# Block-causal attention with a feed-forward layer on one core: rows first, heads second, in the loads of the first batch's q and k

## The chip, the cores and the metric

The kernel runs on one core of a Trainium2 chip. The metric is the device time of one execution in microseconds (us), as the median of several runs. One further execution was recorded by the hardware profiler; all rows below come from it.

## The reference

```python
# q, k, v: (8, 8, 576, 64) float32;  w_in: (512, 2048), w_out: (2048, 512)
scores = (q @ k^T) / sqrt(64)
mask   = (row // 64) >= (column // 64)          # causal in blocks of 64
attn   = softmax(where(mask, scores, -1e9))
x      = (attn @ v), heads side by side          # (4608, 512)
h      = x @ w_in
out    = (h * clip(h + 3, 0, 6) / 6) @ w_out     # (4608, 512)
```

## The kernel before

The work is cut into 32 slots: 8 batches times 4 pairs of heads. A slot's attention runs in 9 blocks of 64 query rows; its two heads sit on the lower and the upper 64 partitions. The feed-forward layer runs beside it, in 12 pieces of 384 tokens, as each piece's attention is finished.

The first four slots (batch 0) are done in float32, all others in split float16. Only the float32 slots are touched here. For each of them q and k are loaded in two parts by `qk_load32`: the first three blocks (192 rows of either head) into a tile `qf`, the other six (384 rows) into a tile `qr`. That makes 16 transfers in all: q and k, two parts, four slots. A partition of the tile holds `nt` neighbouring rows of one head (3 in `qf`, 6 in `qr`). In the kernel before, head 0 fills partitions 0 to 63 and head 1 partitions 64 to 127.

`qk_prep32` turns q and k, so that the 64 features lie on partitions: for each of the `nt` rows of a partition and each head, one product of that head's 64 partitions with a 64x64 piece of the identity matrix `ident`, written with a step of `nt` columns into a PSUM tile (`qt_0`, `qt_1` from `qf`; `qt_0r`, `qt_1r` from `qr`; the names carry 1 for k and 0 for q). A copy then moves the PSUM tile to `qkf`, from which the scores `sf` are computed (`s_pair32`), the softmax rows `pf`, their transposes `pt`, and the products with v, which also carry the name `pf` (`pv_group32`).

All transfers go through the queue of SyncE (SP), except a few of the first ones, which ScalarE issues. The weights arrive in 32 transfers of 512 KB into staging tiles (`rawi`, `rawo`, or a part of `x`), and ScalarE, GpSimd and VectorE turn them into float32 there (`exi`, `exo`, `sgi`, `sgo`) before they are split. The tile `qf` has two buffers, so the third slot's load of `qf` waits for the first slot's products.

The order of the instructions on each engine is fixed by a written-out table; the steps `AS`, `RT` and others only name the places. Every recorded operation carries the line L414 (the recorder's `emit`), so that the rows below are told apart by the names of tiles. On TensorE 40 products with a tile of zeros (`warm`) are spread over the first stretch.

Of the kernel before, what the change touches and what calls it, by code (L numbers as in the profile page):

```python
# [17 lines left out]
P = 128  # L18
# [29 lines left out]
AQ = ("sync", "scalar")  # L48
# [23 lines left out]
BLK = 64  # L72
# [345 lines left out]
def kernel(  # L418
# [113 lines left out]
    ident = wpool.tile([P, P], F32, tag="ident", name="ident")  # L532
# [309 lines left out]
    def qk_load32(n, rest=False):  # L842
        nt = NTR if rest else NTA
        if rest:
            t = natp.tile([P, 2, nt, D], F32, tag="qk", bufs=2, name=f"qr{n}")
        else:
            t = attp.tile([P, 2, nt, D], F32, tag="vhl", bufs=2, name=f"qf{n}")
        c0, c1 = (T0, S) if rest else (0, T0)
        for s, src in enumerate((q, k)):
            nc.load(  # L850
                t[:, s].rearrange("p t d -> p (t d)"),
                src[0, 2 * n:2 * n + 2, c0:c1].rearrange("h (p t) d -> h p (t d)", t=nt), AQ,
            )
        qn[n] = t

    def qk_prep32(n, rest):


        t = qn.pop(n)
        if not rest:  # L860

            if n < 3:
                o = attp.tile(
                    [P, 2 * S], F32, tag="qks" if n == 2 else "qkT", bufs=1 if n == 2 else 2,
                    name=f"qkf{n}",
                )
                qkT[n] = o[:, :S], o[:, S:]
            else:
                qkT[n] = [
                    attp.tile([P, NJ * 2 * P], F16, tag="phl2", bufs=3, name=f"qkf{n}_{i}").bitcast(F32)[:, :S]  # L870
                    for i in range(2)
                ]
        kT, qT = qkT[n]
        c0, c1 = (T0, S) if rest else (0, T0)
        pss = []
        for s in (1, 0):
            if rest and not QTH:
                ps = ps_s.tile([P, 512], F32, tag="s", name=f"qt{n}_{s}r")
            else:
                ps = ps_h.tile([P, S - T0], F32, tag="h", name=f"qt{n}_{s}")  # L880
            nt = NTR if rest else NTA
            nc.joint = "qt", n, s, rest
            for u in range(nt):
                for h in range(2):
                    hb = slice(h * BLK, (h + 1) * BLK)
                    nc.tensor.matmul(
                        ps[hb, u:nt * BLK:nt], t[hb, s, u], ident[hb, hb], start=True, stop=True
                    )
            nc.joint = None
            pss.append(ps)  # L890
        nc.scaled(kT[:, c0:c1], pss[0][:, :c1 - c0], 1.0, "AV")
        nc.scaled(qT[:, c0:c1], pss[1][:, :c1 - c0], D ** -0.5, "AV")
# [671 lines left out]
    def line(points, x):  # L1564

        for (x0, y0), (x1, y1) in zip(points, points[1:]):
            if x <= x1 or (x1, y1) == points[-1]:
                return y0 + (y1 - y0) * (x - x0) / (x1 - x0)
# [7 lines left out]
    for n in range(NPAIR):  # L1576
        t = AS[n]
        at(t, qk_load32, n, lead=AL)
        at(t, v_load, n, lead=AVL)
        at(t, qk_prep32, n, 0)  # L1580
        for b in ((0,), (1, 2)):
            at(t + (1 + b[0]) * U, s_pair32, n, *b)
        for i in range(GB):
            at(t + (1 + i) * U + TA, t_block32, n, i)
        at(t + GB * U + TA + PV0, pv_group32, n, 0)

    for n in range(NPAIR):
        t = RT[n]
        at(t - QR, qk_load32, n, True, lead=RL - QR)
        at(t - QR, qk_prep32, n, 1)  # L1590
        at(AS[3] + 0.1 + 0.1 * n, v_max, n)
        for i in range(2 * GB):
            if i % 2 == 0:
                at(t + i * RS, s_pair32, n, GB + i, GB + i + 1)
            at(t + i * RS + TR, t_block32, n, GB + i)
        for g in (1, 2):
            at(t + (g * GB - 1) * RS + TR + PR, pv_group32, n, g)

    for n in range(NPAIR, NSLOT):
        t, d = line(AT, n), line(AT, n + 1) - line(AT, n)  # L1600
# [97 lines left out]
```

## Time and profile before

| what | value |
|---|---|
| median of 3 runs | 1001.54 us (1000.66 to 1006.18) |
| the profiled execution, its own time | 1003.29 us |
| its span, from the first to the last instruction | 1001.5 us |
| TensorE busy | 964.0 us (96%) |
| VectorE busy | 834.5 us (83%) |
| ScalarE busy | 658.6 us (66%) |
| GpSimd busy | 124.7 us (12%) |
| mean granted TensorE clock | 0.984 of 2.4 GHz |

The span is shorter than the execution's time by 1.8 us, which lie around the first and the last instruction. Busy shares are averages over the span. TensorE's idle time, 37.5 us in all, is not spread evenly: the page's slices of 25 us show it to be mostly in the first five.

### The profile page before, as it was taken

The page shows a single profiled execution, that of the slowest core. Times are in us where ns is not written, and L with a number is a line of the kernel's source. Part 1 is how long each engine was busy: PE and PEld are TensorE (multiplying, and loading weights), DVE is VectorE, ACT ScalarE, POOL GpSimd, SP SyncE. Part 2 cuts the span into 40 slices and gives each one's busy share as a digit, 9 for nine tenths or more (in the row PEclk, how much of TensorE's full clock was granted, in tenths as well). Part 3 has the DMA queues.
Part 4 walks back from the last instruction along what each step waited for, and adds up shares of the span by engine and source line. Part 5 has one row for each costly group of instructions (what it writes and reads, how often), then busy time and mean ns, then how long its engine had stood idle before and what let it go on. Part 6 is the DMA issues. An engine that isn't in the chain of part 4 may idle for free.

```text
span 1001.5 us, 31335 instructions
## 1 busy us (share of the span) xinstructions
PE 964.0 (96%) x12625; PEld 676.5 (68%) x12625; DVE 834.5 (83%) x2366; ACT 658.6 (66%) x1638; POOL 124.7 (12%) x337
## 2 busy tenths in 40 slices
PE   4878999999999999999999999999999999999998
PEld 3656676667777867666667766776666666677775
DVE  1666889999899989999988888989887798978774
ACT  1665889997787887878766676677766553243422
POOL 1343641100001000000001000100100101000000
PEclk7997999999999999999999999999999999999999
DMA  2667677888979998889998968795895550000000
GB/s 86 184 201 214 192 142 141 158 144 172 178 128 177 196 184 141 161 174 162 152 161 145 150 125 143 144 158 117 134 170 100 96 100 17 2 33 3 33 3 33
DMA packets 406706, 129.05 MB, mean 129 GB/s; under 512 B 393504, under 2 KB 396064, under 8 KB 406560
## 3 DMA queue, kind: packets, MB, share of 16 engines
q1 hardware_dynamic: 405628, 126.59, 65.9%
q8 instruction: 99, 1.62, 0.7%
q10 hardware_dynamic: 932, 0.46, 0.2%
q14 instruction: 47, 0.39, 0.1%
HBM read 45.09 MB, written 9.44 MB: 54 GB/s over the span
## 4 chain that ended last, share of the span: by engine, by line
PE 73%; DMA 3%; DVE 2%; ACT 1%; issue 0%; SPq 0%; ACTq 0%; DVEq 0%
PE o L414 31%; PE h L414 25%; PE s L414 6%; PE m L414 5%; PE pv L414 5%; DMA pT<-phl 1%; DMA qkT<-qks 1%; DVE g L414 0%; DMA vnat<-in_v_dram 0%; SPq L414 0%; DMA out_dram<-osb 0%; DVE p L414 0%; PE o_2b L414 0%; ACT p L414 0%; DVE r L414 0%
## 5 line engine op out<-in xcount | busy, mean ns | idle before, releaser
L414 PE MATMUL o<-wout,g 128*64 128x512 f16 (+2 forms) x3336 | 416.5, 379 | 0.4 <-ACT osb L414 0.4
L414 PE MATMUL h<-x,win 128*64 128x384 f16 (+2 forms) x3952 | 363.4, 319 | 2.3 <-DVE hu L414 1.6
L414 PEld LDWEIGHTS <-win 128*64 128x64 f16 (+1 forms) x4440 | 244.4, 110 | 85.5 <-DVE hu L414 1.9
L414 PEld LDWEIGHTS <-g 128*64 128x64 f16 x3360 | 193.8, 110 | 119.2 <-issue 0.6
L414 ACT ACTIVATE r<-h,eg,sh 128x384 f32<-128x384 f32 (+1 forms) x192 | 112.3, 597 | 88.8 <-PE h L414 83.3
L414 ACT ACTIVATE p<-p,st 128x128 f32<-128x128 f32 (+8 forms) x252 | 139.1, 553 | 32.6 <-DVE st L414 31.8
L414 DVE SCALAR_TENSOR_TENSOR phl<-p,st,phl 128x256 f16<-128x256 f32 (+4 forms) x252 | 145.8, 588 | 6.2 <-ACT phl L414 4.6
L414 DVE CUSTOM_DVE_ANT_0 p<-s,none,esc 128x64 f32<-128x64 f32 (+7 forms) x252 | 120.3, 486 | 15.3 <-PE s L414 11.2
L414 DVE SCALAR_TENSOR_TENSOR g<-r,g 128x384 f16<-128x384 f32 (+1 forms) x192 | 105.6, 554 | 9.9 <-ACT g L414 8.5
L414 ACT ACTIVATE phl<-p,st 128x128 f16<-128x128 f32 (+4 forms) x166 | 95.3, 593 | 22.1 <-DVE st L414 18.1
L414 DVE SCALAR_TENSOR_TENSOR r<-r,eg,h 128x384 f32<-128x384 f32 (+1 forms) x160 | 93.6, 587 | 15.8 <-ACT r L414 15.1
L414 PE MATMUL s<-qkT 128*64 128x512 f16 (+7 forms) x1120 | 99.8, 287 | 0.3 <-DMA qkT<-qks 0.3
L414 PEld LDWEIGHTS <-vhl 128*64 128x64 f16 x1680 | 73.0, 110 | 18.0 <-issue 2.2
L414 PE MATMUL pv<-pT,vhl 128*64 128x192 f16 (+2 forms) x1680 | 82.7, 233 | 1.5 <-DMA pT<-phl 1.4
L414 ACT ACTIVATE g<-r 128x384 f16<-128x384 f32 (+1 forms) x109 | 53.5, 497 | 34.0 <-DVE r L414 15.7
L414 PEld LDWEIGHTS <-qkT 128*64 128x64 f16 x1120 | 55.8, 110 | 25.6 <-issue 0.8
L414 POOL MEMSET p<- 128x64 f32 x140 | 20.7, 163 | 327.5 <-DVE phl L414 288.8
L414 ACT ACTIVATE r<-hf,eg,sh 128x192 f32<-128x192 f32 (+1 forms) x48 | 26.8, 593 | 49.8 <-DVE hf L414 49.6
L414 ACT ACTIVATION_READ_ACCUMULATOR p<-p,st 128x1 f32 x252 | 47.7, 189 | 0.0
L414 DVE SCALAR_TENSOR_TENSOR qks<-qk,rs_q,qks 128x576 f16<-128x576 f32 x56 | 45.5, 815 | 0.7
L414 PE MATMUL m<-x,ws 128*64 128x192 f16 x768 | 39.7, 246 | 0.0
L414 PEld LDWEIGHTS <-ws 128*64 128x64 f16 x768 | 34.0, 110 | 5.5 <-issue 0.2
(206 smaller groups left out, 1110.8 us busy)
## 6 DMA issues: line engine op xcount, KB each, us to landing
out_dram<-osb SPq DMA_DIRECT2D x34, 256.0 KB
vnat<-in_v_dram SPq DMA_DIRECT2D x63, 128.0 KB
qk<-in_q_dram SPq DMA_DIRECT2D x28, 288.0 KB
qk<-in_k_dram SPq DMA_DIRECT2D x28, 288.0 KB
rawo<-in_moe_w_out_dram SPq DMA_DIRECT2D x13, 512.0 KB
x<-in_moe_w_in_dram SPq DMA_DIRECT2D x9, 512.0 KB
rawi<-in_moe_w_in_dram SPq DMA_DIRECT2D x7, 512.0 KB
pT<-phl SPq DMA_TRANSPOSE x140
```

The lines of the kernel that those rows point to most:

```text
L414: getattr(eng, method)(*args, **kw)
```

## The change

Both edits concern the first batch alone. The load names the rows' dimension ahead of the heads': the partition of row group p of head h becomes 2p + h, where it was 64h + p. A transfer moves the same bytes in the same number of pieces. The products that turn q and k then take all 128 partitions of the tile, and choose the head by the columns of the identity matrix: every second one, beginning with h. A product with the identity's columns of one head has zeros for the rows of the other.

```diff
@@ qk_load32
         for s, src in enumerate((q, k)):
             nc.load(
                 t[:, s].rearrange("p t d -> p (t d)"),
-                src[0, 2 * n:2 * n + 2, c0:c1].rearrange("h (p t) d -> h p (t d)", t=nt), AQ,
+                src[0, 2 * n:2 * n + 2, c0:c1].rearrange("h (p t) d -> p h (t d)", t=nt), AQ,
             )
@@ qk_prep32
                 for h in range(2):
                     hb = slice(h * BLK, (h + 1) * BLK)
                     nc.tensor.matmul(
-                        ps[hb, u:nt * BLK:nt], t[hb, s, u], ident[hb, hb], start=True, stop=True
+                        ps[hb, u:nt * BLK:nt], t[:, s, u], ident[:, h:P:2], start=True, stop=True
                     )
```

The order of instructions on every engine and every queue is the same before and after; only the operands of the 16 transfers and of the 384 products differ.

## Rows read from the trace of the kernel before

**Rows 1.** The page: span, TensorE's busy time, clock in 40 slices of 25 us.

```profile
span 1001.5 us, 31335 instructions
...
PE 964.0 (96%) x12625; PEld 676.5 (68%) x12625; DVE 834.5 (83%) x2366; ACT 658.6 (66%) x1638; POOL 124.7 (12%) x337
...
PEclk7997999999999999999999999999999999999999
```

**Rows 2.** Timeline of TensorE, 0 to 130 us: groups that begin after idle time.

```profile
start us, us, engine line op out<-in xcount [idle before <-releaser]
1.05 3.83 PE L414 MATMUL warm<-zero 128*128 128x256 f16 x19 [1.05 <-DVE zero L414]
15.43 1.55 PE L414 MATMUL qt<-ident,qf 64*64 64x64 f32 x24 [10.55 <-DMA qf<-in_q_dram]
17.55 0.80 PE L414 MATMUL qt<-ident,qf 64*64 64x64 f32 x10 [0.57 <-DMA qf<-in_k_dram]
...
24.02 0.56 PE L414 MATMUL qt<-ident,qf 64*64 64x64 f32 x12 [1.21 <-DMA qf<-in_q_dram]
...
29.49 0.91 PE L414 MATMUL qt_1r<-ident,qr 64*64 64x64 f32 x24 [1.76 <-DMA qr<-in_k_dram]
...
34.70 1.29 PE L414 MATMUL qt<-ident,qf 64*64 64x64 f32 x24 [2.94 <-DMA qf<-in_q_dram]
...
53.16 0.92 PE L414 MATMUL qt_1r<-ident,qr 64*64 64x64 f32 x24 [2.44 <-DMA qr<-in_k_dram]
...
60.81 0.43 PE L414 MATMUL pr<-rd,halves 128*128 128x64 f32 x2 [3.15 <-POOL rd L414]
...
84.04 1.54 PE L414 MATMUL qt_0r<-ident,qr 64*64 64x64 f32 x24 [4.12 <-DMA qr<-in_q_dram]
...
113.62 0.91 PE L414 MATMUL qt_0r<-ident,qr 64*64 64x64 f32 x24 [1.56 <-DMA qr<-in_q_dram]
```

**Rows 3.** Windows: engines' busy us (x instructions), then clock, DMA share, GB/s.

```profile
2.00:3.00 1.00, 1.00 (x7) 0.69 (x6) 0.00 (x0) 0.07 (x1) 0.06 (x1) 1.00 0.79 155
...
5.00:11.00 6.00, 0.00 (x0) 0.00 (x0) 0.00 (x0) 0.00 (x0) 0.00 (x0) 0.73 0.13 49
...
13.00:15.00 2.00, 0.00 (x0) 0.00 (x0) 0.00 (x0) 0.00 (x0) 0.00 (x0) 0.50 0.97 253
...
84.00:95.00 11.00, 10.96 (x111) 9.09 (x112) 5.29 (x12) 5.76 (x13) 6.75 (x9) 0.59 0.54 163
...
115.00:1001.50 886.50, 878.45 (x11715) 612.48 (x11715) 770.59 (x2160) 593.39 (x1465) 80.47 (x251) 1.00 0.68 123
15.00:115.00 100.00, 81.73 (x892) 61.42 (x893) 63.42 (x204) 63.91 (x172) 42.86 (x73) 0.88 0.61 186
```

**Rows 4.** DMA issues of the tiles `qr` and `qf`, size of one.

```profile
qr<-in_q_dram SPq DMA_DIRECT2D x4, 192.0 KB
...
qf<-in_q_dram SPq DMA_DIRECT2D x3, 96.0 KB
```

**Rows 5.** Timeline of the SP queue: start and duration of issues.

```profile
2.23 0.52 SPq L414 DMA_DIRECT2D qf<-in_q_dram  x1
2.79 5.92 SPq L414 DMA_DIRECT2D qf<-in_k_dram  x1
...
70.84 0.53 SPq L414 DMA_DIRECT2D qr<-in_k_dram  x1
71.41 0.51 SPq L414 DMA_DIRECT2D qr<-in_q_dram  x1
```

**Rows 6.** Timelines of GpSimd and of ScalarE: groups that begin after idle time.

```profile
59.19 0.64 POOL L414 TENSOR_SCALAR sgi<-rawi 128x512 int32<-128x512 uint32 x1 [6.23 <-DMA rawi<-in_moe_w_in_dram]
...
85.26 0.68 ACT L414 ACTIVATE exi<-x 128x512 f32<-128x512 f32 x1 [4.88 <-DMA x<-in_moe_w_in_dram]
...
94.85 0.42 ACT L414 ACTIVATE r<-h,three 128x192 f32<-128x192 f32 x1 [3.44 <-PE h L414]
```

**Rows 7.** Timeline of TensorE, cut to the first products of two groups.

```profile
53.16 0.41 PE L414 MATMUL qt_1r<-ident,qr 64*64 64x64 f32 x7 [2.44 <-DMA qr<-in_k_dram]
...
73.63 0.45 PE L414 MATMUL pf<-pT,vnat 128*64 128x64 f32 x8
```

## The prediction

> **What bounds the kernel now.** I read the page first. TensorE is busy for 96% of the span, and its clock, in slices of 25 us, is below full only in the first four [rows 1]. So the long remainder is TensorE's own work: the window from 115 us to the end has 886.5 us with 878.45 of them busy [rows 3]. Nothing there hangs on an absolute time, so whatever the first 115 us lose or gain should pass to the end one for one. The window from 15 to 115 us is another regime: TensorE is busy for 81.73 us of 100, at 0.88 of its clock, with VectorE at 63.42 and ScalarE at 63.91 [rows 3]. No engine fills it; something is waited for.
>
> The timeline of TensorE says what. After the first `warm` products, which end at 1.05 + 3.83 = 4.88 us, it waits 10.55 us for `qf`. Then come 0.57, 1.21, 1.76, 2.94, 2.44, 4.12 and 1.56 us, each for a `qf` or a `qr`, and 3.15 us for GpSimd [rows 2]. The last of these belongs to the same family: GpSimd, in order, had itself stood 6.23 us for a weight transfer until 59.19, and TensorE's wait ended at 60.81 [rows 2, 6]. Together they are 28.3 us; the whole span has 37.5 us in which TensorE is idle.
>
> Why are transfers of 96 and 192 KB [rows 4] so late? Between 5 and 11 us the share of the 16 DMA engines that is busy is 0.13 at 49 GB/s, while several transfers stand queued. Two engines of sixteen are 0.125. Shortly after, with weights and v in the queue, the same core moves 253 GB/s at 0.97 [rows 3]. So I read the row as: one of these transfers runs on two engines, at about 24.5 GB/s each, and the other fourteen have nothing to do. The issuing queue is held up too: the fourth SP issue takes 5.92 us where the one before took 0.52 [rows 5].
>
> The Trainium skill has a rule that would make this so: by "DMA: Bandwidth & Descriptors", section "Why a DMA increments its semaphore by 16 and not by 1", the number of engines is the largest number up to 16 that divides the slowest dimension on both sides. With heads slowest that is 2, with row groups slowest (64 against 128 partitions) 16. The 0.13 agrees with the 2; nothing in this trace shows the 16 for such a load. The sum below would be zero if the rule's second half did not hold; that is a rival.
>
> **The change part by part.** The load. Two heads slowest becomes 64 row groups slowest, with the same bytes and pieces. Until the first `qt`, five such transfers have to move (four of 96 KB and one of 192 KB, 590 thousand bytes): 12.0 us at 49 GB/s, 2.3 us at 253 GB/s. For the pair of `qr` issued at 70.84 and 71.41 [rows 5], 393 thousand bytes, it is 8.0 us against 1.6, and in the old form it also makes the weights behind it late, since each of their transfers waits for its share on the two busy engines.
>
> First wait. The last `qf` of slot 0 is issued at 2.23 + 0.52 us. The trace has no landing of such a transfer on all engines. As a lower bound stands TensorE's end of `warm`, 4.88; as an upper one 2.75 + 2.3 for the bytes + 1.5 for the start, 6.5 (the first transfers of all, v's, are seen moving between 2 and 3 us, so a start takes no longer than about that [rows 3]). I take 5.2, near the lower end, because the three other transfers need not all be through. Gain: 15.43 - 5.2 = 10.2 us (8.9 to 10.5).
>
> Waits on `qf` and `qr`. From 17 to 35 us they are 0.57 + 1.21 + 1.76 + 2.94 = 6.5 us; later 2.44 + 4.12 + 1.56 = 8.1; with GpSimd's 3.15 the sum is 17.75 us [rows 2]. Each lands 2 to 8 us earlier by the sums above, which is more than any of the waits. For the largest: the second `qr` of the pair was issued 84.04 - 71.41 = 12.6 us ahead of its use; after 1.6 us of transfer and even 3 us of queueing it lies ready at 76, four us before TensorE's idle time begins at 79.92. I count all 17.75.
>
> The clock. It stands at half (1.2 GHz) after idle stretches: 0.88 over 100 us at two levels is 24 us at half clock, so 12 us is the most that it can give back [rows 3]. From 84 to 95 us, behind the 4.12 us wait, it is 0.59 with TensorE busy for 10.96 us, which loses 10.96 x 0.41 = 4.5 us; there ScalarE waits 3.44 us for TensorE's `h` [rows 3, 6], so TensorE sets the pace and I count them. Of the remaining 7.5 much lies under other engines' work; I count 1.5. Sum 6 (0 to 12).
>
> Waits that take their place. With 18 + 6 us gone from the 100, ScalarE's 63.91 and VectorE's 63.42 us [rows 3] have to fit into 76: 84%, with work that depends on each other. Some waits must appear; the trace doesn't price them. Bounds: 0, and 12, half of what has gone. What is late next is the weights' conversion on ScalarE: its 4.88 us for `x` [rows 6] shrinks only as far as that transfer comes earlier. I take 4.
>
> The products. There are 384, in 192 pairs, one for either head. They go from 64 rows by 64 columns to 128 by 64, with a moving operand of the same 64 columns taken at a step of two. The nearest row: seven products of 64x64 take 0.41 us, eight of 128x64 with 64 float32 columns, at the same full clock, 0.45 [rows 7]. That is one product more for 0.04 us, no dearer. They can no longer share the array with `sf`, which also uses 64 rows; I allow 1 us in all (0 to 4). The step of two has no row.
>
> The sum, in the profiled execution's time: 10.2 + 17.75 + 6 - 4 - 1 = 29 us from 1003.3, so 974.3. The median of the runs shown is 1.75 us below that execution, so 972.5. The bounds: 8.9 + 17.75 + 0 - 12 - 4 = 10.7 at the worst, 10.5 + 17.75 + 12 = 40 at the best. All ends together are unlikely; 21 to 38 us, 963.5 to 980.5, is the likeliest case's own range.
>
> **The rivals.** *The waits re-form.* The stretch from 15 us on is held by ScalarE, VectorE and the weights' staging buffers, and only the first wait and part of the rest are kept: 10 to 21 us, 980.5 to 991.5. For it: both engines busy for 64 us of 100 around TensorE's waits. Against: ScalarE's long waits in rows 6 are themselves for transfers or for a TensorE at half clock. *Still two engines.* Should the transfer be cut by heads as before, nothing moves but the products: 1001 to 1003. Against it stands only that the order of dimensions is what differs from loads that use all engines. *More than summed.* SP no longer stalls, so weights come earlier than TensorE's gain, and the clock never falls: 38 to 46 us, 955.5 to 963.5.
>
> *Slower.* The 128-row products lose the overlap of weight load and product. Were each of 384 to pay 0.135 us for its own load, that would be 52 us against the 29 + 1 gained without it: 1024. It turns the change into a loss from 30 / 384 = 0.08 us per product on. Against it: rows 7, where 128x64 pairs run as closely as 64x64. A rule of the skill would make it happen: "TensorE: Matmul & The Clock Gate", section "Part 3: Packing small matmuls — row/col tiling", says that a weight load overlaps running products only when the row group differs, and the heads now share theirs. Rows 7 speak against this rule for column tiles. A milder form, a moving operand at half rate for its step of two, would cost some 192 x 0.06 = 11 us: 983.5, within the first rival's span.
>
> **How the numbers follow.** Likeliest case 0.70; waits re-form or the step of two is dear 0.17; more than summed 0.06; still two engines 0.04; slower 0.03. The predicted time is the likeliest's, 972.5. For 8 in 10 the range takes in the likeliest and the nearer half of both neighbours: 961 to 986. Half a per cent, 5 us, is about what a measurement here can tell from no change: faster 0.93, same 0.04, slower 0.03.
>
> **What would show it.** After the change the DMA share of the first 5 us should be well above 0.13 and no stretch before 11 us should sit at it; the first `qt` should start near 5.2 us; SP's fourth issue should take about 0.5 us; TensorE's waits for `qf` and `qr` should be gone, GpSimd's for `rawi` with them; the clock from the first `qt` to the end near 1.00; the last 886 us unchanged in length. A group of 24 `qt` products at full clock should still take about 0.92 us. The prediction is wrong if the share stays at 0.13, if `qt` groups lengthen, or if equal waits on ScalarE and VectorE stand where the DMA waits were.

## The result and the profile after

The changed kernel takes 967.9 us in the median of 4 runs (967.08 to 969.72); the kernel before takes 1001.51, in 4 runs too. The ratio is 0.9658 with a 95% interval of 0.9625 to 0.969: 33.6 us less, and inside the forecast range. The profiled execution has a span of 967.9 us, 33.6 less than before.

The page of the kernel after (span, busy us, TensorE's clock in 40 slices), which answers to [rows 1]:

```profile
span 967.9 us, 31335 instructions
...
PE 956.5 (99%) x12625; PEld 665.2 (69%) x12625; DVE 837.8 (87%) x2366; ACT 658.4 (68%) x1638; POOL 124.6 (13%) x337
...
PEclk9999999999999999999999999999999999999999
```

The same instructions run; TensorE's busy time is 7.5 us less, and its clock no longer falls after the start. The timeline of TensorE, 0 to 100 us, with all groups that begin after an idle time that the view shows, answers to [rows 2]:

```profile
1.05 4.24 PE L414 MATMUL warm<-zero 128*128 128x256 f16 x19 [1.05 <-DVE zero L414]
5.47 0.92 PE L414 MATMUL qt<-ident,qf 128*64 128x64 f32 x24 [0.18 <-DMA qf<-in_q_dram]
6.67 0.57 PE L414 MATMUL qt<-ident,qf 128*64 128x64 f32 x12 [0.28 <-DMA qf<-in_k_dram]
...
23.25 0.46 PE L414 MATMUL pt<-ident,pf 128*128 128x128 f32 x2 [0.28 <-ACT rb L414]
...
48.85 0.19 PE L414 MATMUL gs<-wm,unit 128*64 128x2 bf16 x2 [0.16 <-DVE wm L414]
...
55.27 0.93 PE L414 MATMUL qt_1r<-ident,qr 128*64 128x64 f32 x24 [0.16 <-DVE dg_w L414]
```

Ten rows have become six, and none of those left is longer than 0.28 us, TensorE's first step aside. The SP queue, 0 to 30 us, answers to [rows 5]:

```profile
2.17 0.61 SPq L414 DMA_DIRECT2D qf<-in_q_dram  x1
2.82 0.61 SPq L414 DMA_DIRECT2D qf<-in_k_dram  x1
3.47 0.60 SPq L414 DMA_DIRECT2D rawi<-in_moe_w_in_dram  x1
```

The issue that took 5.92 us takes 0.61, and the weights' first transfer follows at 3.47. Windows show the rest (engines' busy us, then clock, DMA share and GB/s). The first row answers to the row of the same 6 us in [rows 3]. The other two divide the kernel after at the last `qt_0r`, the group that starts behind the last of the waits of before (113.62 us there): the 861 products from the first `qt` up to it, and all from it on:

```profile
5.00:11.00 6.00, 5.53 (x107) 4.20 (x107) 3.27 (x19) 2.33 (x9) 1.00 (x3) 1.00 0.80 251
...
5.50:78.70 73.20, 72.22 (x861) 53.54 (x861) 64.55 (x202) 62.46 (x169) 41.79 (x72) 1.00 0.84 257
...
78.70:967.90 889.20, 879.97 (x11746) 608.89 (x11745) 772.78 (x2162) 594.65 (x1469) 81.50 (x253) 1.00 0.67 123
```

The kernel before, over the same 861 products and over the rest:

```profile
15.40:113.60 98.20, 80.35 (x861) 60.17 (x862) 63.38 (x203) 63.91 (x172) 42.86 (x73) 0.88 0.61 187
...
113.60:1001.50 887.90, 879.82 (x11745) 613.73 (x11745) 770.63 (x2160) 593.39 (x1465) 80.47 (x251) 1.00 0.68 123
```

This is the whole account. The stretch begins 15.4 - 5.5 = 9.9 us earlier. It is 98.2 - 73.2 = 25.0 us shorter: idle time falls from 17.85 to 0.98 us (16.9), and busy time for the same products from 80.35 to 72.22 us (8.1), at a clock of 1.00 in place of 0.88. The rest is 889.2 - 887.9 = 1.3 us longer here; the part on the prediction's steps shows a second execution in which it is not. 9.9 + 25.0 - 1.3 = 33.6.

### The profile page after: what moved, and what is told of

It reads as the page before. It is cut to its first block, busy times and chain, and to the rows that moved or that the text cites. A ratio compares the mean times of both kernels' runs of the same rounds, so it can differ in the third digit from the quotient of the medians.

```text
span 967.9 us, 31335 instructions
## 1 busy us (share of the span) xinstructions
PE 956.5 (99%) x12625; PEld 665.2 (69%) x12625; DVE 837.8 (87%) x2366; ACT 658.4 (68%) x1638; POOL 124.6 (13%) x337
## 2 busy tenths in 40 slices
DMA packets 406930, 129.05 MB, mean 133 GB/s; under 512 B 393728, under 2 KB 396288, under 8 KB 406784
## 4 chain that ended last, share of the span: by engine, by line
PE 66%; DMA 2%; DVE 2%; ACT 1%; issue 0%; SPq 0%; POOL 0%; ACTq 0%; DVEq 0%
PE o L414 29%; PE h L414 22%; PE m L414 5%; PE s L414 5%; PE pv L414 4%; DMA qkT<-qks 1%; DMA vnat<-in_v_dram 1%; DMA pT<-phl 1%; DVE p L414 0%; DVE g L414 0%; DVE r L414 0%; DMA out_dram<-osb 0%; DVE phl L414 0%; DVE qks L414 0%; ACT r L414 0%
```

## The experiments

The theory: the gain comes from the number of DMA engines that carry one of the 16 transfers, 2 before and 16 after; the products play no part. The rivals: the layout or the products bring or cost something, or waits re-form elsewhere. Times beside each other share runs of the kernel before.

**Rows first, but on few engines.** The changed kernel, each transfer cut in two at a row group m, whose divisors limit the engines (m = 62, 57, 63):

```diff
+            to = t[:, s].rearrange("p t d -> p (t d)")
+            rows = src[0, 2 * n:2 * n + 2, c0:c1].rearrange("h (p t) d -> p h (t d)", t=nt)
+            nc.ops[-1].ways = {
+                e: [("dma_start", (to[2 * a:2 * z], rows[a:z]), {}) for a, z in ((0, m), (m, BLK))]
+                for e in AQ
+            }
```

*m = 62.*

> The change with each of the 16 transfers cut at row group 62 of 64 (62 has no divisor up to 16 except 2 and 1): layout and products of the change, nearly all bytes again on two DMA engines if the number of engines is set by the slowest dimension. Theory (the number of engines is the cause): 999 to 1007 us, the DMA share at 0.13 for most of 5 to 11 us, the first qt after 15 us. Rival (layout or products bring the gain): 966 to 972 us.

Measured: 1000.41 us against 1002.63 for the kernel before; ratio 0.9979 (0.996 to 0.9997). The timeline of TensorE and the window from 5 to 11 us:

```profile
15.08 1.55 PE L414 MATMUL qt<-ident,qf 128*64 128x64 f32 x24 [10.45 <-DMA qf<-in_q_dram]
...
84.93 0.93 PE L414 MATMUL qt_0r<-ident,qr 128*64 128x64 f32 x24 [4.23 <-DMA qr<-in_q_dram]
```

```profile
5.00:11.00 6.00, 0.00 (x0) 0.00 (x0) 0.00 (x0) 1.28 (x1) 0.00 (x0) 0.69 0.13 48
```

With the new layout and the new products (128x64 in the row), the share of 0.13 is back and all but 2 us of the gain is gone. Layout and products are not the cause, and no cost of theirs shows either: from the first `qt` to the last `qt_0r`, which starts at 113.13 us, it is 98.1 us, 98.2 before.

*m = 57.*

> As the run before, cut at row group 57, whose largest divisor up to 16 is 3. Theory: transfers take two thirds of the time that they take on two engines, so the first five land at about 11 us (590 thousand bytes at 73.5 GB/s is 8.0 us), DMA share near 0.19 there; 4 us less of first wait, most of the shorter waits gone, some of the clock: 978 to 988 us. Rival (only a transfer on all engines helps, since the slow share still sets the landing): 996 us or more.

Measured: 983.1 us, ratio 0.9814 (0.9791 to 0.9836). The first `qt` starts at 10.32 us, 5.1 us earlier than before; the waits on `qf` and `qr`, the first included, come to 12.0 us. The waits of TensorE, 0 to 120 us (total, times, longest):

```profile
PE qt L414 <- DMA qf<-in_q_dram: 6.6, 2, 5.0
PE pr L414 <- POOL rd L414: 3.0, 2, 1.7
PE qt_1r L414 <- DMA qr<-in_k_dram: 2.4, 1, 2.4
PE qt_0r L414 <- DMA qr<-in_q_dram: 2.3, 1, 2.3
...
PE qt L414 <- DMA qf<-in_k_dram: 0.7, 1, 0.7
```

Without the first wait of 5.0 us and with the one for GpSimd, 10.0 us of the shorter waits stay, of 17.75 before; that most of them would go did not come true, though the time did. The DMA share over 5 to 11 us is 0.32, because other transfers are under way in part of it. In a stretch where it stands flat it is 0.20 at 69 GB/s, near the expected 0.19 and 73.5 GB/s:

```profile
8.00:9.50 1.50, 0.00 (x0) 0.00 (x0) 0.00 (x0) 0.00 (x0) 0.00 (x0) 1.00 0.20 69
```

*m = 63.*

> Cut at row group 63, largest divisor up to 16 is 9; the last row group goes alone on one engine. Theory: five transfers need 2.7 us in place of 12.0, every wait but a part of the first is covered: 967 to 973 us. Rival (the gain grows with every engine up to 16): above 976 us.

Measured: 971.7 us, ratio 0.9705 (0.9682 to 0.9728). The first `qt` starts at 7.80 us; one wait of 0.96 us and one of 0.31 are the only ones after 10 us that the timeline marks.

The number of engines can be counted in the traces. ScalarE's queue (`q10`) carries two of the 16 transfers, whole or cut, and beside them the same work in every kernel. Its packets, MB and share, in the kernel before, in the changed kernel, and for m = 62, 57 and 63:

```profile
q10 hardware_dynamic: 932, 0.46, 0.2%
q10 hardware_dynamic: 960, 0.46, 0.2%
q10 hardware_dynamic: 936, 0.46, 0.2%
q10 hardware_dynamic: 948, 0.46, 0.2%
q10 hardware_dynamic: 950, 0.46, 0.2%
```

For each of the two transfers that is 14 packets more than before in the changed kernel, and 2, 8 and 9 more with the cuts. Over all queues the changed kernel has 406930 packets for 406706, again 14 for each of 16, all of them under 512 B and with the same bytes in all. If a transfer adds one short packet for every engine that carries it, which no run isolates, and used 2 before, it uses 16 now, and the two parts of a cut one together 4, 10 and 11. That fits 2 + 2, 3 + 7 (57 and 7 row groups) and 9 + 2. By this count the larger parts ran on the numbers of engines that were expected, and the last row group of m = 63 on two and not on one.

With nearly all row groups on 2, 3 and 9 engines, and all on 16, the time is 1000.4, 983.1, 971.7 and 967.9 us (the last from the runs of the result): the step from 2 to 3 brings half the gain. All nine waits of before but the first were under 4.2 us, so a transfer that lands a few us earlier can already cover part of each. The cut kernels are flattered by some 4 us, though: behind the last `qt_0r` they take 883.5 to 884.0 us, where the kernel before takes 887.9, with fewer short waits there. Why was not tried. Up to that product the dose shows more clearly: it starts at 113.13, 97.97, 84.06 and 78.72 us.

**Heads first, but on all engines.** The kernel before, with its 64x64 products, each load as two transfers:

```diff
+            op = nc.ops[-1]
+            op.ways = {
+                e: [
+                    ("dma_start", (
+                        t[h * BLK:(h + 1) * BLK, s].rearrange("p t d -> p (t d)"),
+                        src[0, 2 * n + h, c0:c1].rearrange("(p t) d -> p (t d)", t=nt),
+                    ), {}) for h in range(2)
+                ] for e in AQ
+            }
```

> The kernel before, with its layout and its 64x64 products, but each load sent as two transfers, one for either head, whose slowest dimension is 64 row groups. Theory (only the engines matter, the products cost and bring nothing): 967 to 973 us, 16 more issues of about 0.55 us costing at most 3 us of it; first qt near 6.5 us. Rival (128-row products bring part of the gain): 975 us or more. Rival (128-row products cost): under 966 us.

Measured: 970.98 us, ratio 0.9699 (0.9678 to 0.972). So nearly all of the gain is to be had without the new layout. The changed kernel's median is 2 to 3 us lower (967.9 and 968.7 in its two sets of runs); whether that is the 16 further issues was not tried. TensorE's timeline begins with the old products at the new time:

```profile
5.26 0.30 PE L414 MATMUL qt<-ident,qf 64*64 64x64 f32 x2 [0.59 <-DMA qf<-in_q_dram]
5.81 1.60 PE L414 MATMUL qt<-ident,qf 64*64 64x64 f32 x33 [0.26 <-DMA qf<-in_q_dram]
```

**The halves of the change.** The new order for `qf` alone, and for `qr` alone:

```diff
-                src[...].rearrange("h (p t) d -> p h (t d)", t=nt), AQ,
+                src[...].rearrange("h (p t) d -> p h (t d)" if not rest else "h (p t) d -> h p (t d)", t=nt), AQ,
...
+                    tt, idn = (t, ident[:, h:P:2]) if not rest else (t[hb], ident[hb, hb])
```

> The change for the first part alone (qf); qr stays heads first, with 64x64 products. Theory: the first qr still holds two engines for its 192 KB (4.0 us at 49 GB/s) ahead of the first slot's q, so the first qt starts near 8.5 us in place of 5.5 (7 us gained of 10); the waits on qf (6.5 us) mostly go; those on qr and the one behind the late weights (1.76, 2.44, 3.15, 4.12, 1.56) stay, with their stretch of half clock: 984 to 993 us. Rival (the first wait is all that matters, later ones re-form): above 990 us with the later waits unchanged and as many as before.

> The change for the second part alone (qr); qf stays heads first. Theory: four transfers of 96 KB need 8.0 us on two engines, first qt near 11.5 us (4 us gained), part of the waits on qf stays, all waits on qr and behind the late weights go, and the half clock from 84 us on with them: 975 to 984 us. Both halves' gains together should come to the whole's 34 us within some 4 us. Rival (the halves are worth little alone, since either leaves two engines blocked): both above 990 us.

> The changed kernel itself, as the base of the runs beside it: 967 to 970 us.

Measured, against 1004.94 us before: `qf` alone 991.47 (ratio 0.9876, 0.9851 to 0.99), `qr` alone 979.1 (0.9754, 0.9731 to 0.9777), both, the changed kernel, 968.68 (0.9649, 0.963 to 0.9669). The halves gain 13.5 and 25.8 us, together 39.3 against 36.3 for the whole. The first two times lie in their forecast ranges. With `qf` alone the wait for the first `qr` (1.76 us before) has become one of 0.80 us for ScalarE, the later ones stand nearly as before:

```profile
9.70 2.27 PE L414 MATMUL qt<-ident,qf 128*64 128x64 f32 x36 [4.41 <-DMA qf<-in_q_dram]
...
41.74 0.91 PE L414 MATMUL qt_1r<-ident,qr 64*64 64x64 f32 x24 [2.50 <-DMA qr<-in_k_dram]
49.50 0.43 PE L414 MATMUL pr<-rd,halves 128*128 128x64 f32 x2 [3.27 <-POOL rd L414]
72.30 1.54 PE L414 MATMUL qt_0r<-ident,qr 64*64 64x64 f32 x24 [3.69 <-DMA qr<-in_q_dram]
101.85 0.92 PE L414 MATMUL qt_0r<-ident,qr 64*64 64x64 f32 x24 [1.40 <-DMA qr<-in_q_dram]
```

That includes GpSimd's `rd`, 3.27 us. It is gone where only `qr` is changed, so it belonged to the `qr` transfers, as the prediction had it. What TensorE waits for there, from 0 to 125 us, without the start (total, times, longest):

```profile
PE qt L414 <- DMA qf<-in_q_dram: 8.4, 3, 6.5
PE qt L414 <- DVE vnat L414: 1.2, 1, 1.2
...
PE pt L414 <- ACT rb L414: 0.4, 1, 0.4
PE qt_1r L414 <- DMA qr<-in_k_dram: 0.3, 1, 0.3
```

The larger half is not the one with the longest single wait: the order of `qr` also sets the first wait, since the first `qr` is issued ahead of the first slot's q. With `qf` alone on all engines the first `qt` still starts at 9.70 us.

**The products of zeros.** The changed kernel without the later 21 of the 40:

```diff
+            if o.eng == "tensor" and "warm" in o.ways["tensor"][0][1][0].tensor.name:
+                seen += 1
+                if seen > 19:
+                    continue
```

> The changed kernel without the 21 later products of zeros (those that before stood in TensorE's idle time between 19 and 30 us). They are not part of the computation. Theory: TensorE has no idle time left there, so 21 products of 256 columns at full clock (about 0.11 us) now lie on its path: up to 2.2 us less, 965.5 to 967.5 us. Rival: they still fill gaps in which TensorE would wait for VectorE and ScalarE, or hold up the clock: no difference, or slower through half clock.

Measured: 967.78 us, ratio 0.9641 (0.962 to 0.9662) beside 0.9649 (0.963 to 0.9669) with them; the intervals overlap. The profiled spans are 967.2 and 967.1 us, and short waits for ScalarE, VectorE and GpSimd stand where the products were (1.2 us for `rd` the longest). By this pair the rival holds, but a gain of up to the 2.2 us forecast is not excluded; the next pair bears on it too.

**The first slot's transfers first,** and 9 leading products of zeros in place of 19, without and with the cut above:

```diff
+        for o in qf0 + [o for o in steps if o not in qf0]:
...
+                if seen > 40 or seen > 9 and seen <= 19:
+                    continue
```

> The changed kernel with the first slot's k and q (qf) as the first issues of their two queues, ahead of v and of the first qr, and with 9 in place of 19 products of zeros before the first qt (they fill no gap any more and are no part of the computation). Theory: the first qt waits for nothing but its own transfer, issued 1.4 us earlier, and all that follows on TensorE's path moves with it: first qt near 3.6 us in place of 5.5, 966 to 967.5 us. Rival (v, qr or the second slot's qf, now later, are waited for instead): 967.5 to 969 us, with a new wait of 1 us or more before 15 us.

> As the run before, and without the 21 later products of zeros as well. Theory (both lie on TensorE's path): 1 us below the run before, 965 to 966.5 us. Rival (they fill gaps): the same as the run before.

Measured, against 1002.68 us before: 970.67 (0.9674, 0.9654 to 0.9695) and 968.07 (0.9655, 0.9636 to 0.9675). Neither ratio is better than the changed kernel's, and the first time lies above both of its forecasts. The second is 2.6 us below the first, and their runs do not overlap (967.77 to 968.71 against 969.11 to 970.87). So here it did bring time to leave out the later products of zeros, more than the 1 us forecast, where the pair before differed by 0.9 us, within its spread. Of the 3.2 us between the two profiled spans (968.9 and 965.7) 2.5 lie behind 79 us, where no such products are (889.6 and 887.1 us); why is open, and so is the price of these products. The start of TensorE's timeline in the first of the two:

```profile
1.05 2.10 PE L423 MATMUL warm<-zero 128*128 128x256 f16 x9 [1.05 <-DVE zero L423]
3.89 1.55 PE L423 MATMUL qt<-ident,qf 128*64 128x64 f32 x24 [0.73 <-DMA qf<-in_q_dram]
6.46 0.91 PE L423 MATMUL qt<-ident,qf 128*64 128x64 f32 x12 [1.02 <-DMA qf<-in_k_dram]
7.29 0.92 PE L423 MATMUL sf<-qkf 64*64 64x128 f32 x8
```

The first `qt` does start 1.6 us earlier. But 24 products take 1.55 us where they take 0.92 in the changed kernel, and the next twelve 0.91 where they take 0.57. The kernel before took 1.55 us for 24 at 15.43 us [rows 2], where its clock column reads 0.50, so the array runs at half clock (1.2 GHz). What it did less of ahead of them are the ten products of zeros. There is also a new wait of 1.02 us for k, the sign that the rival had named. By 12 us the head start has turned into a delay: the third group of 24 `qt`, here and then in the changed kernel:

```profile
12.00 0.92 PE L423 MATMUL qt<-ident,qf 128*64 128x64 f32 x24
...
10.35 0.93 PE L414 MATMUL qt<-ident,qf 128*64 128x64 f32 x24
```

## Why the prediction was right, step by step

| term | forecast, us | measured, us | where |
|---|---|---|---|
| first wait | 10.2 (8.9 to 10.5) | 9.9 | first `qt` at 5.47 for 15.43, windows cut at 5.5 and 15.4 |
| waits on `qf`, `qr` and the late weights | 17.75 | 17.5 | two transfer waits are left, 0.18 and 0.28; the first counts in the line above |
| clock | 6 (0 to 12) | 8.1 | 80.35 busy us become 72.22, same products |
| waits in their place | -4 (0 to -12) | -0.6 | 0.28 + 0.16 + 0.16 for ScalarE and VectorE |
| products | -1 (0 to -4) | 0 | 24 in 0.92 us before and after |
| the rest of the kernel | 0 | -1.3 | 887.9 us become 889.2; 887.9 in a second execution |
| sum | 29 | 33.6 | span; the median gives 33.6 too |

*Two engines.* Right, and shown: with all else changed but the engines held at two, all but 2 us of the gain is away; with nothing changed but the engines, and twice the issues, all but 2 to 3 us of it is there. The rule of the Trainium skill ("DMA: Bandwidth & Descriptors", "Why a DMA increments its semaphore by 16 and not by 1") let the three cuts be chosen by their divisors. The share of 0.13 at m = 62 and of 0.20 at m = 57 and the packet counts of all three cuts agree with it.

*The waits.* All seven, but for 0.28 us of the first, and the one behind GpSimd went as forecast. The forecast reason fits: in the kernel after, a `qr` lands 3.3 to 5.3 us after its issue, and the last two, issued at 64.8 and 70.9 us, are first used at 72.08 and 78.72. The forecast's own sum was loose here: 2 us, the lower end of what it let a transfer land earlier, is less than three of the waits.

*Two terms were mis-sized, both on the cautious side.* The clock gave back 8.1 us, two thirds of its bound of 12, where I had counted half. The waits in their place were the larger miss in kind: ScalarE and VectorE did fill up as forecast (from 5.5 to 78.7 us 62.46 and 64.55 of 73.2, 85% and 88%), yet TensorE waited for them for 0.6 us and not 4. A share of busy time that high does not by itself mean waiting. The likely reason, not tested, is that the written-out order interleaves attention and feed-forward work, so that an engine has something else to do while a result is late.

*The remainder is unmoved within what executions differ by.* In the account above it is 1.3 us longer than before. A second profiled execution of the changed kernel (span 967.1 us) has it at 887.9 us, as before, and then the 861 products from the first `qt` take 0.7 us more:

```profile
5.30:79.20 73.90, 72.04 (x861) 53.43 (x861) 63.33 (x202) 62.09 (x169) 42.47 (x72) 1.00 0.82 255
79.20:967.10 887.90, 879.86 (x11746) 616.96 (x11745) 772.62 (x2162) 594.78 (x1469) 82.17 (x253) 1.00 0.68 123
```

So these runs do not show the 1.3 us to be a price of the change. In the other profiled executions this stretch takes 886.8 to 889.6 us, in the three cut kernels 883.5 to 884.0. What moves about are short waits, as for a transpose by DMA (`pT`): the longest of this kind stands at 256.57 us in the kernel before and at 338.28 us, at other products, in the first execution of the kernel after.

```profile
256.57 0.93 PE L414 MATMUL pv<-pT,vhl 128*64 128x192 f16 x18 [1.19 <-DMA pT<-phl]
...
338.28 0.44 PE L414 MATMUL pv<-pT,vhl 128*64 128x192 f16 x6 [1.20 <-DMA pT<-phl]
```

The same spread holds for the terms above that are of this size: in the second execution TensorE waits 0.5 us for VectorE and 0.7 for a transfer of v.

*The rival that would have made it slower.* Weight loads of products that share their rows did not stand in the way. In the kernel after, a group of 24 products of 128x64 takes 0.92 us at full clock, as one of 64x64 did in [rows 2], and a weight load for `qt` takes 136 ns in the median (the least, the median and the most, in ns):

```profile
L414 PEld LDWEIGHTS qt<-ident,qf x96: 132/136/153, 5.4 to 17.4; 128*64 128x64 f32 x96
```

By that median 24 loads one behind the other would take 3.3 us, and even two at a time 1.6. The rule of the Trainium skill ("TensorE: Matmul & The Clock Gate", "Part 3: Packing small matmuls — row/col tiling") that loads overlap running products only where row groups differ does not hold for these pairs on two column groups. The moving operand's step of two costs nothing either, by the same row. *The waits re-form* did not happen. With three engines the time, 983.1 us, lies in this rival's range, but for another reason: 10.0 us of waits on the same transfers and for GpSimd stayed, and those on ScalarE and VectorE came to 1.3.

## What to carry to other kernels

Read the DMA share of a short window in which few transfers are queued: a flat value at a small multiple of a sixteenth while something waits (0.13 and 0.20 here) was the sign of a transfer on few engines. The order of dimensions, or one transfer per head, then brought 32 to 36 us; the one reordering of the queue that was tried, on top of that, brought nothing. Such a transfer made others late too, those that queue behind it on the same engines and the issues behind it on its queue, so look for its price in the waits of other tiles, and in the clock after them. Once the idle time is gone, what filled it (here products of zeros) has to be judged anew, by trying it.

## What the runs showed of the hardware beyond this

The leading products of zeros matter for the clock, at a start that looks warm. With 19 of them (4.24 us) the first 24 `qt` take 0.92 us, with 9 (2.10 us) 1.55 us; the order of the first transfers differs too, so this is the likely cause and not a separate test. The clock column reads 1.00 all along in both, here in the changed kernel from 1 to 3 us:

```profile
1.00:3.00 2.00, 1.95 (x10) 1.40 (x11) 0.31 (x2) 0.48 (x1) 0.93 (x8) 1.00 0.48 107
```

Yet these 19 products of 256 columns take 4.24 us, 0.22 each. Seven of the same later in the same trace take 0.13 each, and seven in the kernel before, from 19.67 us on, where the column reads 0.50, take 0.24:

```profile
13.06 0.93 PE L414 MATMUL warm<-zero 128*128 128x256 f16 x7
...
19.67 1.68 PE L414 MATMUL warm<-zero 128*128 128x256 f16 x7
```

So the first ones run at half clock. At the start of these executions the durations tell the clock, and the column does not.
